# A packed attention with FFN: the last four pairs of units of batch 1 by seven block products, signs of weights with one operand, and a new order of the early steps

## The chip, the cores and the metric

The kernel runs on one core of one Trainium2 chip. The time is the device time of one execution in microseconds; the comparison is between the medians of several executions of either kernel on the same chip.

## What is computed

Eight batches of eight heads, 576 tokens of 64 elements a head. A first attention lets 32 packs a head attend to the tokens; a second lets the tokens attend to the packs. The result, 4608 tokens of 512 elements, goes through an FFN of width 2048 with a gated activation, all in float32:

```python
def _attn_ref(q, k, v, p):
    p_packed = sm_attn(p, k, v)
    out = sm_attn(q, p_packed, p_packed)

def _moe_ref(x, w_in, w_out):
    h = x @ w_in
    g = h * (1.0 / (1.0 + np.exp(-h)))
    return (g @ w_out).astype(np.float32)
```

The kernel never forms the attention's result: it multiplies the packs by w_in first ("packs", one matrix of 128x512 a parity and quarter of the FFN) and then multiplies these by the shares of the second softmax.

## The kernel before, in words

**Weights.** w_in and w_out arrive as 64-bit numbers in 20 chunks (eight of 512 columns, one FFN block each; twelve of 1024), on SP's queue (`Weights.fetch`, L269). Each is put together as float32 from its upper and lower words: ScalarE scales the upper word (`scale`, L283) and rounds the lower (`round`, L287), VectorE bounds the upper (`bound`, L291), puts the sign into the lower (`sign`, L295), shifts (`shift`, L303), and VectorE or GpSimd adds the two (`join`, L306). w_out is then split into an upper and a lower part (`upper`, `lower`). w_in stays in `win`, four quarters.

**A product in float32** is made of three faster products, upper by upper, upper by lower, lower by upper. The first three units of batch 0 (`WHOLE`) use plain float32 matmuls instead, so that no splits are needed yet.

**Units.** A unit is one batch and one block of 128 of the FFN's 2048. `h_products` (L797) multiplies packs by shares, `h_values` (L813) applies the gated activation, `h_lower` (L848) makes the lower part, and `out_part` or `out_products` multiply by w_out and add up in `ps_acc` over a batch's units (L853 to L914). 256 of a half's 288 tokens go through a unit; the other 32 are put aside in `rest` and have units of their own. Units 0 to 31 are those of batches 0 and 1, in the order of `BLOCKS`: batch 0's first two quarters, batch 1's first two, batch 0's last two, batch 1's last two (units 24 to 31). Units 32 to 35 are the rest of both; from unit 36 on the batches follow one another.

**Seven block products.** From batch 2 on, two neighbouring units form a pair (`Seven`, L677): two blocks of the FFN by two halves of the tokens by two parities is a product of 2x2 matrices of blocks, and seven products in place of eight give it. For this, sums and differences of blocks of the packs are made in place (`sums`, L693; step `mv` on VectorE, `mp` on GpSimd), split (`parts`, L704, step `mh`), and the shares get block differences of their own (`blocks2`, `parts2`, steps `aP`, `aQ`). Steps H, I, J, K, L (L733 to L757) issue the seven products into three banks of `ps_one`, with copies on ScalarE and additions on VectorE between them; A and B (`values`, L761) apply the activation to the even and the odd half.

**Packs.** `Packs.products` (L635) makes a quarter's packs. With `kept` (L659) they are stored over the quarter of `win` that they came from, and `split` (L665) makes upper and lower parts from there; `packs_split` (L1000, step `Kd`) makes the parts straight from PSUM and stores nothing. Before that the first half of each quarter of w_in is copied to `spare` in DRAM (step `c`) and is loaded again (step `wb`) for the next batch's packs.

**PSUM.** Up to step `za` there are two tiles of two banks for scores and units (`ps_two`); from there on four single banks (`ps_one`). Four banks are `ps_acc`. Step `zb` frees the weights' staging room for `late`, `odd`, `gp_b` and `s1p`.

**The order** is written out by hand as a string, `ORDER` (L54): each step names a helper and its numbers, and each engine, SP's queue included, takes its instructions in that order. `W` are warm-up matmuls; `k`, `v`, `q` load a batch's inputs; `as` to `aj` are the first attention, `aS` to `aL` the second; `w.` the weights (`wf` fetch, `ws`, `wr`, `wz`, `wg`, `wt`, `wj` in the order of the sentence above, `wu` and `wl` the split); `pp`, `pu`, `pl` packs and their split; `h`, `g`, `l`, `o` a unit; `O` one output block; `e` storing a batch's rows; `b` loading partial sums. `SEVENS` says which pairs of which batch go by sevens.

Of the kernel before, what the change touches and what calls it, by code (L numbers as in the profile page):

```python
# [1090 lines left out]
```

## Time and profile before

| | before |
|---|---|
| median of 3 runs | 677.47 us (677.41 to 678.12) |
| the profiled execution's own time | 677.38 us |
| its span | 675.6 us |
| TensorE, VectorE, ScalarE, GpSimd busy | 666.2, 447.5, 461.1, 75.4 us |
| LDWEIGHTS busy | 542.8 us |
| DMA | 77.76 MB, mean 115 GB/s |

PE is TensorE, PEld its loading of weights, DVE VectorE, ACT ScalarE, POOL GpSimd, SP the engine that issues the DMAs. Busy time is the time in which an instruction of that engine runs. Matmuls are pipelined and their ends are modelled: two neighbouring rows can overlap, and the distance between their starts is the better measure. Releasers of waits are inferred from semaphores. Line numbers are those of the kernel before. The granted clock of TensorE is 1.00 in every stretch shown.

### The profile page before, as it was taken

The numbers are of one execution on the slowest core, as the hardware profiler recorded it, in microseconds if no ns is written. First come the engines' busy times: TensorE is split into PE (matmuls) and PEld (weight loads), VectorE is DVE, ScalarE is ACT, GpSimd is POOL, SyncE is SP. The second block draws the span as 40 slices with busy tenths as digits, with TensorE's granted clock in tenths as the row PEclk, the third lists the DMA queues.
The fourth block names the chain that finished last, engine by engine and source line by source line (L and its number), as shares of the span: only waits on it lengthen the run. The fifth ranks groups of instructions, "written<-read, shape, count | busy, mean of one in ns | idle before, by whom it ended". The sixth has DMA issues, their size and how long they took to land.

```text
span 675.6 us, 12742 instructions
## 1 busy us (share of the span) xinstructions
PE 666.2 (99%) x4920; PEld 542.8 (80%) x4920; DVE 447.5 (66%) x784; ACT 461.1 (68%) x1060; POOL 75.4 (11%) x79
## 2 busy tenths in 40 slices
PE   8999999999999999999999999999999999999997
PEld 5558888868888778886888868887788868888886
DVE  3999977656655788655685479755668566955431
ACT  4999786555648686765777578766677657776542
POOL 1122013110300000211001220212002101001000
PEclk9999999999999999999999999999999999999999
DMA  9966527605214420247011320184202330110002
GB/s 356 420 225 251 198 103 216 244 1 205 104 64 141 147 108 1 65 143 268 18 62 52 95 103 1 40 260 146 85 26 74 84 121 1 31 64 1 1 0 79
DMA packets 31916, 77.76 MB, mean 115 GB/s; under 512 B 17136, under 2 KB 17136, under 8 KB 27504
## 3 DMA queue, kind: packets, MB, share of 16 engines
q1 hardware_dynamic: 31760, 76.82, 32.3%
q8 instruction: 39, 0.64, 0.4%
q10 hardware_dynamic: 96, 0.13, 0.1%
q14 instruction: 21, 0.17, 0.1%
HBM read 59.77 MB, written 13.63 MB: 109 GB/s over the span
## 4 chain that ended last, share of the span: by engine, by line
PE 95%; DMA 3%; ACT 2%; issue 0%; DVE 0%; SPq 0%; ACTq 0%
PE ps_acc L862 59%; PE ps_one L730 20%; PE ps_two L811 5%; PE ps_one L338 5%; PE ps_one L811 2%; DMA win<-in_w_in 2%; PE ps_two L338 1%; PE ps_one L434 1%; DMA kvq_t<-in_pkT 1%; PE ps_two L434 0%; ACT win L663 0%; ACT s L369 0%; ACT L840 0%; PE ps_two L408 0%; ACT pw_hi L672 0%
## 5 line engine op out<-in xcount | busy, mean ns | idle before, releaser
L862 PE MATMUL ps_acc<-wo_hi,g_hi 128*128 128x512 f32 x564 | 223.1, 396 | 0.0
L862 PE MATMUL ps_acc<-wo_lo,g_hi 128*128 128x512 f32 x564 | 221.0, 392 | 0.0
L862 PE MATMUL ps_acc<-wo_hi,g_lo 128*128 128x512 f32 x564 | 220.1, 390 | 0.0
L862 PEld LDWEIGHTS ps_acc<-wo_hi,g_hi 128*128 128x128 f32 x564 | 105.9, 188 | 23.5 <-issue 8.6
L862 PEld LDWEIGHTS ps_acc<-wo_hi,g_lo 128*128 128x128 f32 x564 | 105.9, 188 | 23.5
L862 PEld LDWEIGHTS ps_acc<-wo_lo,g_hi 128*128 128x128 f32 x564 | 105.9, 188 | 14.0
L748 DVE TENSOR_TENSOR top<-ps_one,top 128x288 f32<-128x288 f32 x48 | 21.8, 455 | 57.1 <-ACT top L747 56.8
L699 POOL TENSOR_TENSOR win<-win 128x256 f32<-128x256 f32 x15 | 12.1, 808 | 421.0 <-DVE pw_lo L673 247.2
L777 DVE TENSOR_TENSOR g_lo<-low,g_hi 128x512 fp32r<-128x512 f32 x48 | 33.9, 707 | 34.5 <-ACT low L769 34.5
L747 ACT COPY top<-ps_one 128x288 f32<-128x288 f32 x48 | 19.1, 398 | 46.8 <-PE ps_one L730 46.6
L743 ACT COPY low<-ps_one 128x288 f32<-128x288 f32 x48 | 19.2, 400 | 34.8 <-PE ps_one L730 33.1
L777 DVE TENSOR_TENSOR g_lo<-top,g_hi 128x512 fp32r<-128x512 f32 x48 | 33.9, 707 | 11.8 <-ACT top L775 10.7
L730 PE MATMUL ps_one<-wide_hi,odd 128*128 128x288 f32 x144 | 38.2, 296 | 0.2 <-ACT top L738 0.2
L774 ACT ACTIVATE g_hi<-top 128x512 fp32r<-128x512 f32 x48 | 30.4, 633 | 11.0 <-DVE top L748 8.8
L755 DVE TENSOR_TENSOR low<-ps_one,low 128x288 f32<-128x288 f32 x48 | 21.7, 452 | 24.2 <-PE ps_one L730 23.1
L851 DVE TENSOR_TENSOR g_lo<-g,g_hi 128x512 fp32r<-128x512 f32 (+1 forms) x30 | 21.5, 716 | 19.3 <-ACT g_hi L836 9.7
L775 ACT ACTIVATE top<-top 128x512 f32<-128x512 f32 x48 | 30.4, 633 | 1.5
L673 DVE TENSOR_TENSOR pw_lo<-win,pw_hi 128x512 fp32r<-128x512 f32 (+1 forms) x50 | 26.6, 557 | 3.2 <-ACT pw_hi L672 2.5
L730 PE MATMUL ps_one<-a_hi,pw_hi 128*128 128x288 f32 x96 | 28.4, 296 | 0.1
L730 PE MATMUL ps_one<-a_hi,pw_lo 128*128 128x288 f32 x96 | 28.2, 294 | 0.0
L730 PE MATMUL ps_one<-a_lo,pw_hi 128*128 128x288 f32 x96 | 28.2, 294 | 0.0
L730 PEld LDWEIGHTS ps_one<-wide_hi,odd 128*128 128x128 f32 x144 | 26.3, 188 | 2.1 <-ACT top L738 0.5
(236 smaller groups left out, 1445.6 us busy)
## 6 DMA issues: line engine op xcount, KB each, us to landing
win<-spare SPq DMA_DIRECT2D x21, 512.0 KB, 3.8
kvq_t<-in_v SPq DMA_DIRECT2D x8, 1280.0 KB, 7.3
kvq_t<-in_pkT SPq DMA_DIRECT2D x7, 1216.0 KB, 10.3
out<-o SPq DMA_DIRECT2D x16, 512.0 KB, 3.1
kvq_t<-in_qT SPq DMA_DIRECT2D x7, 1152.0 KB, 6.3
w_raw<-in_w_in SPq DMA_DIRECT2D x6, 1024.0 KB, 9.1
win<-in_w_out SPq DMA_DIRECT2D x3, 1024.0 KB, 6.2
w_raw<-in_w_out SPq DMA_DIRECT2D x3, 1024.0 KB, 6.8
```

The costliest lines, as they stand in the source:

```text
L338: nc.tensor.matmul(bank(par)[NP * i : NP * i + NP], lhs(r, i), rhs(r, i), start=True, stop=True)
L673: nc.vector.tensor_tensor(some_lo, some, some_hi.bitcast(F32), ALU.subtract)
L730: nc.tensor.matmul(bank, x, y, start=(first and n == 0), stop=(n == 2), skip_group_check=True)
L743: nc.scalar.copy(self.low[:, 0], self.x)
L748: nc.vector.tensor_tensor(self.top[:, 1], self.z, self.top[:, 1], ALU.add)
L755: nc.vector.tensor_tensor(self.low[:, 0], self.z, self.low[:, 0], ALU.add)
L774: nc.scalar.activation(g_hi.rearrange("p (n s) -> p n s", n=2), g, AF.Silu)
L775: nc.scalar.activation(g, g, AF.Silu)
L777: nc.vector.tensor_tensor(g_lo.rearrange("p (n s) -> p n s", n=2), g, g_hi.bitcast(F32).rearrange("p (n s) -> p n s", n=2), ALU.subtract)
L811: nc.tensor.matmul(bank, p[:, par, cols] if u >= WHOLE else p[:, par], a[:, par], start=(n == 0), stop=(n == len(todo) - 1))
L851: nc.vector.tensor_tensor(g_lo[:, c], g[:, c], g_hi[:, c].bitcast(F32), ALU.subtract)
L862: nc.tensor.matmul(bank, g[:, rows], w[:, at], start=(first and n == 0), stop=(last and n + 1 == len(todo)))
```

## The change

The pairs of units 24 to 31 of batch 1 go by seven block products. For that the third quarter's packs of batch 1 are kept, in a tile of `s1p` and not over `win`, so that this quarter needs no new load for batch 2. Batch 1 gets the sums of its shares' parts (step `aR1`) and their block differences (`aP1`, `aQ1`). `sign` becomes an operation with one operand on 16-bit words. The order is another one up to the middle of batch 2 (686 steps of before become 699); from step `aH3.1` in batch 3 on it is the same, 1003 steps.

```diff
-SEVENS = [()] * EARLY + [range(8)] * (B - EARLY)
+SEVENS = [(), range(4, 8)] + [range(8)] * (B - EARLY)

+    def room_of_packs(b, j):
+        if b >= EARLY or j != 2:
+            return over_win(j).bitcast(F32)
+        if ("room", b) not in made:
+            made["room", b] = s1p.tile([P, 2 * S], F32, name="s1")[:, : 2 * DM].rearrange("p (r e) -> p r e", r=2)
+        return made["room", b]

+            halves = raw.bitcast(U16).rearrange("p (n four) -> p four n", four=4)
+            self.halves[n] = halves[:, 1], halves[:, 3]

         def sign(self, n):
-            low, up = self.raw[n]
-            nc.vector.scalar_tensor_tensor(low, up, -(2**31), low, op0=ALU.bitwise_and, op1=ALU.bitwise_or)
+            low, up = self.halves[n]
+            nc.vector.tensor_scalar(low, up, 2**15, None, op0=ALU.bitwise_and)

-            self.whole = [over_win(j)[:, par].bitcast(F32) for par in range(2)]
+            self.whole = [room_of_packs(self.b, j)[:, par] for par in range(2)]
...
-            elif self.n < 4 or self.n == 5 and self.b < EARLY:
+            elif self.n < 4:
                 t = s1p.tile([P, 2 * S], F32R, name="s1")[:, : 2 * DM]
```

`sums` and `parts` use `room_of_packs` in the same way. Of the order, the first lines and the stretch from step `za` to batch 2's first pair, before:

```
W7 k0 as0.0 W1 wf0 v0 as0.1 am0.0 am0.1 W4 ax0.0 W3 W1 W1 wr0 at0.0 ay0.0 ax0.1 ar0 at0.1 ws0 wz0 wt0 wg0 wj0 ay0.1
wf1 wr1 aa0 an0 ai0 aj0 q0 wf2 wf3 W1 aS0.0 ws1 wz1 wg1 wt1 wj1 aC0.0 aS0.1 aC0.1 aB0.0 ws2 wr2 wf4 aB0.1 aM0.0 aE0.0
aX0.0 pp0 aM0.1 pu0 k1 wf5 wr4 W14 wf6 aD0.0 wf7 ws3 ws4 aE0.1 aG0.0 wf8 aX0.1 wz2 aD0.1 wr3 aU0.0 aF0.0 aH0.0 as1.0
ac1.0 wt2 aG0.1 wg2 h0.0 as1.1 aU0.1 wj2 g0.0 wz4 wg4 ws6 wz3 aF0.1 wf9 wt3 pp1 q1 wg3 wj3 pu1 ws5 wt4 ac1.1 am1 wj4
wr6 wz6 o0.0 h1.0 g1.0 ws8 wz5 wt5 v1 wz8 aL0.0 wt6 wr5 wg5 wg6 h0.1 g0.1 h1.1 g1.1 wj5 o1.0 o0.1 ax1.0 ax1.1 at1.0
...
aj2 za O20.0.0 O20.1.0 O20.1.1 Kp1.3 Ke1.3 Kp1.2 wu19 O20.0.1 O21.0.0 wl19 zb h22 g22 b0 l22 Kd1.2 O21.0.1 h23 O21.1.1
g23 q2 aS2.0 aT2.0 aY2 Kp2.0 Ke2.0 Kp2.1 Ke2.1 l23 Kp2.2 aM2.0 aS2.1 Ke2.2 O22.0.0 aT2.1 O22.1.1 h24 O21.1.0 h25
...
O36.0.0 O36.1.1 O37.0.0 O36.1.0 k4 wb2.0 ax3.0 ax3.1 O36.0.1 L38 O37.1.1 O38.0.1 at3.0 K38 at3.1 O37.0.1 ar3 O39.1.0
```

and after:

```
W7 k0 as0.0 as0.1 W4 W3 v0 am0.0 wf0 ax0.0 am0.1 W1 W1 at0.0 ay0.0 ax0.1 at0.1 ar0 ay0.1 aa0 an0 ws0 wz0 ai0 wr0 wg0
wt0 wj0 q0 aj0 aS0.0 wf1 wf2 aC0.0 aS0.1 aC0.1 wf3 W1 ws1 aB0.0 aM0.0 aE0.0 k1 pp0 pu0 aB0.1 W14 aX0.0 aM0.1 wf4 wf5
wf6 wr2 aD0.0 aG0.0 aE0.1 ws2 wz2 wg2 wf7 aU0.0 wr3 wt2 wz1 wj2 wt1 ws3 wr1 wg1 wj1 aF0.0 aX0.1 aH0.0 as1.0 ac1.0
as1.1 ac1.1 aD0.1 aG0.1 wr4 wz3 pp1 pu1 ws5 wz5 h0.0 wt3 wt5 g0.0 h1.0 g1.0 wf8 aU0.1 ws4 wz4 wt4 wg4 aF0.1 wg3 wj3
wr7 wj4 am1 q1 aL0.0 ws7 wz7 wg7 wr5 wg5 o0.0 h1.1 wj5 g1.1 h0.1 ws6 wz6 wt6 pp2 g0.1 pu2 ax1.0 o1.0 wt7 wj7 ax1.1 ar1
h2.0 at1.0 ws8 ay1.0 wz8 wr8 o0.1 at1.1 o1.1 v1 wg8 ay1.1 aa1 wf9 wt8 wj8 an1 g2.0 h2.1 wr6 wu7 wg6 wj6 ws9 wl7 ai1
...
wl19 h21 o19 g21 l21 za O20.1.0 aR1 aP1 h22 O20.0.0 zb g22 l22 Kp1.2 Ke1.2 aQ1 Kp1.3 O21.1.0 Ke1.3 O20.1.1 h23 Ks1.2
O20.0.1 O22.1.1 g23 l23 b0 q2 aS2.0 aT2.0 mv1.4 Kp2.0 Ke2.0 aS2.1 aT2.1 O21.1.1 mh1.4 O22.1.0 O23.1.0 O23.1.1 e23.1
Kp2.1 Kp2.2 Ke2.1 aM2.1 Ke2.2 aY2 aM2.0 H24 I24 O22.0.1 J24 aE2.0 Ks1.3 O21.0.0 O21.0.1 L24 K24 O22.0.0 aE2.1 O23.0.0
A24 mh1.5 B24 O23.0.1 H26 I26 e23.0 O25.1.0 O25.1.1 aX2.0 J26 mv1.6 O24.1.1 O24.0.0 aX2.1 O24.0.1 O24.1.0 A26 O25.0.1
O25.0.0 L26 aD2.0 mh1.7 mh1.6 K26 O27.1.1 O26.0.0 B26 H30 I30 O26.0.1 aG2.0 O27.1.0 J30 O27.0.1 O26.1.1 L30 A30 aD2.1
K30 B30 H28 O27.0.0 O31.1.1 I28 O30.1.1 O31.0.0 aG2.1 J28 aH2.1 aL2.1 O31.0.1 O30.1.0 wb2.3 aH2.0 aL2.0 O30.0.1 L28
...
Kp2.3 Ke2.3 Ks2.3 ar3 k4 aV3 mv2.6 an3 ac4.0 ac4.1 mh2.5 O42.0.1 H44 I44 O41.0.1 ai3 aj3 J44 O40.1.1 O40.1.0 q3 L44
O43.1.0 am4 O42.0.0 K44 O42.1.0 A44 mh2.6 O42.1.1 wb2.0 wb2.1 B44 aS3.0 aT3.0 Kp3.1 aY3 Ke3.1 Kp3.0 Ke3.0 aM3.0 wb2.2
```

## Rows read from the trace of the kernel before

**Rows 1.** The page: busy us, share of the span and instructions of each engine.

```profile
PE 666.2 (99%) x4920; PEld 542.8 (80%) x4920; DVE 447.5 (66%) x784; ACT 461.1 (68%) x1060; POOL 75.4 (11%) x79
```

**Rows 2.** Waits of TensorE from 24 to 675 us: us in total, times, longest.

```profile
PE ps_two L453 <- ACT g_hi L840: 0.7, 1, 0.7
PE ps_one L730 <- ACT top L738: 0.2, 1, 0.2
```

**Rows 3.** Timeline of TensorE near 166 us: start us, duration us, what.

```profile
165.97 0.39 PE L862 MATMUL ps_acc<-wo_hi,g_lo 128*128 128x512 f32 x1
166.20 0.29 PE L811 MATMUL ps_one<-a_hi,pw_hi 128*128 128x288 f32 x1
166.33 0.29 PE L811 MATMUL ps_one<-a_lo,pw_hi 128*128 128x288 f32 x1
```

**Rows 4.** Busy us by stretch: PE, PEld, DVE, ACT, POOL, clock, DMA share, GB/s.

```profile
20.00:30.00 10.00, 8.69 (x81) 5.10 (x80) 9.45 (x18) 9.57 (x18) 1.18 (x1) 1.00 1.02 417
30.00:40.00 10.00, 10.00 (x127) 5.98 (x126) 8.70 (x21) 9.97 (x21) 1.63 (x2) 1.00 0.86 335
```

**Rows 5.** Groups of VectorE by line and shape: busy us, mean ns of one.

```profile
L748 DVE TENSOR_TENSOR top<-ps_one,top 128x288 f32<-128x288 f32 x48 | 21.8, 455 | 57.1 <-ACT top L747 56.8
...
L715 DVE TENSOR_TENSOR odd<-win,odd 128x512 fp32r<-128x512 f32 x24 | 16.5, 687 | 2.1 <-ACT odd L714 1.7
...
L699 DVE TENSOR_TENSOR win<-win 128x256 f32<-128x256 f32 x9 | 3.8, 418 | 0.0
...
L617 DVE TENSOR_TENSOR tm<-tm 128x288 f32<-128x288 f32 x6 | 3.2, 528 | 0.2
```

**Rows 6.** Busy us by stretch, two later stretches, columns as in rows 4.

```profile
140.00:200.00 60.00, 60.00 (x407) 49.51 (x406) 39.56 (x61) 32.32 (x82) 6.87 (x8) 1.00 0.28 105
240.00:260.00 20.00, 20.00 (x153) 15.29 (x138) 17.88 (x35) 16.54 (x36) 0.00 (x0) 1.00 0.09 29
```

**Rows 7.** Timeline of all engines in the first 24 us.

```profile
3.82 0.44 SPq L247 DMA_DIRECT2D rest<-in_qT  x1
...
6.17 0.77 PE L232 MATMUL ps_two<-ident 128*128 128x128 f32 x2
...
6.87 0.72 PE L338 MATMUL ps_acc<-kvq_t 64*32 64x288 f32 x16
...
7.71 0.33 SPq L238 DMA_DIRECT2D kvq_t<-in_pkT  x1
...
9.41 0.67 ACT L289 ACTIVATE w_raw<-w_raw 128x512 int32<-128x512 uint32 x1
...
9.97 0.73 ACT L389 ACTIVATE tm<-ps_acc,nm 128x576 f32<-128x576 f32 x1
...
14.71 0.77 PE L338 MATMUL ps_acc<-rest,ppT 64*32 64x320 f32 x16
...
20.09 0.90 DVE L540 TENSOR_TENSOR tm<-ps_acc,on_tokens 128x768 f32<-128x768 f32 x1
...
20.90 0.68 DVE L574 TENSOR_TENSOR tm<-tm,on_tokens 128x512 f32<-128x512 f32 x1
...
22.81 0.72 PE L338 MATMUL ps_two<-kvq_t 64*32 64x288 f32 x16 [0.46 <-ACT w_raw L289]
```

**Rows 8.** Issue to landing in the first 45 us: queries (L247), then keys (L238).

```profile
DMA to landing us min/median/max: 9.8/10.3/10.8
...
DMA to landing us min/median/max: 4.0/5.0/15.0
```

**Rows 9.** Lines of sign (L297) and bound (L293): ns min/median/max, first and last start, shapes.

```profile
L297 DVE SCALAR_TENSOR_TENSOR w_raw<-w_raw x13: 686/1224/1244, 12.3 to 130.1; 128x1024 int32<-128x1024 int32 x9, 128x512 int32<-128x512 int32 x4
...
L293 DVE TENSOR_SCALAR w_raw<-w_raw x13: 422/687/694, 11.4 to 129.4; 128x1024 f32<-128x1024 f32 x9, 128x512 f32<-128x512 f32 x4
```

**Rows 10.** The page's DMA issues: count, KB each, median us to landing.

```profile
win<-spare SPq DMA_DIRECT2D x21, 512.0 KB, 3.8
...
kvq_t<-in_qT SPq DMA_DIRECT2D x7, 1152.0 KB, 6.3
```

More of the change, by code (lines that the diff above doesn't have):

```diff
@@ L13 @@
 U32 = mybir.dt.uint32
+U16 = mybir.dt.uint16
 I64 = mybir.dt.int64
@@ new lines @@
+O69.0.1 J72 O70.1.0 g71 l71 O70.1.1 L72 O70.0.1 A72 O70.0.0 O71.0.0 mh4.1 K72 O71.0.1 B72 wb4.0 O71.1.0 H74 I74
+O73.1.1 O72.1.1 J74 O71.1.1 O73.1.0 e71.0 L74 O72.0.1 O72.0.0 O73.0.1 ay5 mh4.2 K74 A74 O74.0.1 B74 H76 mh4.3 I76
+O74.0.0 O72.1.0 wb4.3 O75.1.1 O75.0.0 J76 O74.1.1 ar5 O73.0.0 O75.1.0 L76 K76 Ks4.2 mp4.4 A76 B76 O75.0.1 H78 O74.1.0
+I78 O77.1.0 O76.0.0 J78 O77.1.1 O76.0.1 L78 wb4.1 A78 K78 B78 O76.1.0 O77.0.1 Kp4.3 Ke4.3 Ks4.3 mp4.6 aV5 mh4.4 an5
+ac6.0 ac6.1 mh4.5 O79.1.1 O79.1.0 am6 H80 I80 ai5 O78.0.1 J80 aj5 O78.0.0 mh4.7 O77.0.0 q5 L80 O76.1.1 K80 A80 B80
@@ new lines @@
+mh5.1 wb5.0 v6 A88 e87.1 O86.0.0 O86.0.1 O87.0.1 e87.0 K88 L88 B88 H90 O88.0.1 O88.0.0 mh5.2 O89.1.0 k7 I90 O89.0.0
+O88.1.0 J90 O89.0.1 O89.1.1 L90 A90 K90 O88.1.1 B90 H92 O90.0.0 mh5.3 I92 O91.0.1 O91.1.1 J92 Ks5.2 mp5.4 O91.1.0
+O90.0.1 L92 O90.1.1 A92 O90.1.0 K92 B92 O91.0.0 H94 I94 O92.1.1 O93.0.1 mh5.4 J94 A94 wb5.3 O92.0.1 O92.1.0 O93.0.0
+L94 K94 O93.1.0 B94 O95.1.0 Kp5.3 Ke5.3 Ks5.3 mp5.6 ay6 aV6 an6 ac7.0 ac7.1 O94.0.0 H96 q6 am7 I96 mh5.5 O95.1.1
+O92.0.0 J96 O95.0.0 ai6 O93.1.1 wb5.1 mh5.7 aj6 L96 O94.1.1 A96 O94.0.1 K96 B96 O97.1.0 O94.1.0 aS6.0 aT6.0 aY6 wb5.2
@@ new lines @@
+O120.0.1 aL7.1 mh7.0 J122 O120.1.1 aH7.0 aL7.0 aP7 O119.0.0 K122 A122 O121.0.1 O121.0.0 O121.1.0 O121.1.1 L122
+O123.1.0 O122.0.1 O122.0.0 aQ7 B122 H124 Ks7.1 I124 O123.0.0 O123.0.1 mh7.1 J124 O120.1.0 O122.1.0 e123.0 K124 L124
+O123.1.1 A124 B124 O122.1.1 H126 e123.1 O125.1.1 mv7.2 I126 O125.1.0 O124.0.1 J126 O124.1.0 O125.0.0 O124.0.0 A126
+L126 mh7.3 mh7.2 O125.0.1 O126.0.0 K126 B126 O127.1.1 H128 I128 Ks7.2 mp7.4 O127.1.0 O124.1.1 J128 O126.1.0 O126.0.1
+L128 A128 K128 O127.0.0 B128 O126.1.1 H130 I130 O129.1.1 O129.0.0 O127.0.1 J130 A130 O128.0.1 O128.0.0 O129.0.1 L130
@@ L141 @@
+e139.0 O139.1.1 l140 O140.1.0 O140.0.0 O140.1.1 g142 l142 O142.0.1 e139.1 O140.0.1 g143 l143 g141 O142.1.1 O143.1.1
+O143.1.0 l141 O141.1.1 O143.0.1 O141.0.0 O141.0.1 O142.1.0 O143.0.0 O142.0.0 O141.1.0 e143.0
 """
-SEVENS = [()] * EARLY + [range(8)] * (B - EARLY)
+SEVENS = [(), range(4, 8)] + [range(8)] * (B - EARLY)
 WAYS = dict(b11=(0, 0), b21=(0, 1), b12=(1, 0), b22=(1, 1), t1=(2, 0), t4=(2, 1), t3=(2, 2), t2=(2, 3))
@@ L266, in __init__ @@
         def __init__(self, stage):
-            self.stage, self.raw = stage, {}
+            self.stage, self.raw, self.halves = stage, {}, {}
         def fetch(self, n):
@@ L279, in fetch @@
             nc.sync.dma_start(raw.bitcast(I64), (w_in if inner else w_out)[:, f * DM : (f + nf) * DM])
-            raw = raw.rearrange("p (n two) -> p two n", two=2)
-            self.raw[n] = raw[:, 0], raw[:, 1]
+            words = raw.rearrange("p (n two) -> p two n", two=2)
+            halves = raw.bitcast(U16).rearrange("p (n four) -> p four n", four=4)
+            self.raw[n] = words[:, 0], words[:, 1]
+            self.halves[n] = halves[:, 1], halves[:, 3]
         def scale(self, n):
@@ L695, in sums @@
                 n = 2 if self.n % 2 == 0 and (self.b, self.n + 1) in sevens else 1
-                both = over_win(self.n // 2).bitcast(F32)[:, :, self.n % 2 * 2 * P : (self.n % 2 + n) * 2 * P]
+                both = room_of_packs(self.b, self.n // 2)[:, :, self.n % 2 * 2 * P : (self.n % 2 + n) * 2 * P]
                 (a11, a21), (a12, a22) = [[both[:, par].rearrange("p (g k n) -> p g k n", g=n, k=2)[:, :, k] for k in range(2)] for par in range(2)]
```

143 lines of the change are left out of this document (56 added, 87 removed).

## The prediction

> **What bounds the kernel now.** I read the profile's page first. TensorE is busy 666.2 of 675.6 us [rows 1], but its matmuls are pipelined and their ends are modelled, so this share alone settles nothing. Next come TensorE's waits from 24 us to the end: 0.7 and 0.2 us, each once, and nothing else [rows 2]. Then the timeline inside a stage: a matmul of 288 columns is followed 0.13 us later by the next one, one of 512 columns 0.23 us later, though each is listed as taking 0.29 or 0.39 us [rows 3]. So from about 23 us on TensorE takes matmuls back to back, and the time is the moment at which that stream starts plus the sum of its spacings. Before it comes a start-up, a chain through batch 0's attention; beside it VectorE and ScalarE are 9.45 and 9.57 of 10 us busy from 20 to 30 us, 8.70 and 9.97 in the next ten [rows 4]. So three things can move the time: fewer matmuls, an earlier start, and new waits of TensorE.
>
> The rule against this reading: LDWEIGHTS takes 542.8 us, 80% of the span [rows 1]. The Trainium skill ("Perfetto Trace Analysis", Identifying the Most-Contended Engine) says that TensorE's matmul occupancy is no measure and that LDWEIGHTS busy share tells its headroom; by that, a fifth of the span is free and a removed matmul need not show. The spacings decide for me: no room stands between matmuls [rows 3].
>
> **Part 1, seven products for pairs of batch 1.** Units 24 to 31 are four pairs. A pair of plain units issues 24 matmuls of 288 columns (2 halves x 2 parities x 3 terms, twice), a pair by sevens 7 x 3 = 21. So 4 x 3 = 12 matmuls go, each worth its spacing, 0.131 us [rows 3]: **-1.57 us**. Output matmuls and the packs' products are as many as before.
>
> What it adds lies on VectorE and ScalarE. On VectorE, per pair: three additions of 128x288 (0.455 each) and one lower part of 128x512 (0.69) [rows 5], 2.05 us, times 4 is 8.2. Two calls of the block sums, four operations of 128x256 at 0.418 each [rows 5]: 3.3. For the shares of batch 1: two additions and two subtractions of 128x576, estimated at 0.77 each by length from 0.69 for 512, 3.1; four block differences at 0.53 [rows 5], 2.1. Together **16.7 us**; the values' lower parts are as many as before, and keeping the third pack instead of splitting it at once adds about nothing, since half a split falls away. ScalarE gets some 8 us (three copies at about 0.4 and one at 0.63 a pair), but from 140 to 200 us it is busy 32.3 of 60, so I price that at nothing; uncovered, a late copy would hold a PSUM bank for at most its own 0.4 us.
>
> VectorE has no such cover. In this stretch, which holds the eight units and the lead-up to batch 2's sevens, it is busy 39.56 of 60 us [rows 6]. The demand becomes 56.3 in 60 - 1.6 = 58.4 us, 96%. The best that rows show over ten busy microseconds is 9.45 of 10 [rows 4]: 56.3/0.945 = 59.6, so TensorE waits **+1.2 us**. The lower end is 0, by 240 to 260 us, where VectorE runs at 17.88 of 20 and TensorE shows no wait [rows 6, 2]; the upper end is +5.6, if it gets no more than 88%. I take the row of the fullest stretch, which this one is nearest to. Queued behind a late VectorE addition are the fourth and fifth products, which go into the banks it reads, and the next pair's first products, which need its lower part.
>
> **Part 2, the start.** The keys' second half takes 5.0 us to land [rows 8]; TensorE then does a warm-up first (6.17) and the scores at 6.87 [rows 7]; the warm-up goes behind them, 0.6 us. ScalarE rounds a w_in chunk (9.41) ahead of the second exponential (9.97) [rows 7]; the rounding goes behind, 0.6 us. The second scores need the queries, issued 3.82, landed 10.8 us later, 14.6, and start at 14.71 [rows 7, 8]. In the new order one w_out chunk of 512 KB is behind them on SP's queue instead of ahead; at 417 GB/s [rows 4] that is 1.26 us. So all three inputs of the second scores come about 1 us earlier. Later, VectorE does half 1's subtraction (20.09) ahead of half 0's scaling (20.90) [rows 7]; exchanged, 0.9 us. Batch 1's keys, issued 7.71, take 15.0 us, 22.7, and their scores start at 22.81 [rows 7, 8]: again one chunk fewer ahead, 21.5.
>
> Against that: the first FFN products now stand behind both of batch 1's scores and the second pack, and that pack needs a weight chunk that VectorE finishes among six weight operations, put ahead of half 1's scaling. So not all of 1.3 to 2 us arrives. I take **-1.0 us**, half of the way from the end -2.0 (every step counts) to 0; the other end is +0.7, if VectorE's six operations (about 0.43 each, 2.6 us) eat more than the start wins.
>
> **Part 3, signs with one operand.** A sign operation with two operands takes 0.69 us for 512 columns, 1.22 for 1024 [rows 9]. No row shows a 16-bit operation with steps of four. The nearest one-operand row with steps is the bound: 0.42 for 512, 0.69 for 1024 [rows 9]. I take that: 8 x 0.26 + 12 x 0.54 = 8.6 us off VectorE up to 130 us, with both ends 0 and that. None lies on TensorE's stream; it pays for the six operations of part 2. The one long wait after 24 us, 0.7 us at the table load for the gated values near 41 us [rows 2], should shrink, since what it waits for moves forward: **-0.5 us**, ends -0.9 and +0.5. The number of table loads stays.
>
> **Moved transfers.** Queries 1 and values 1 pass the w_out chunk 9, which lands some 6 us later (1.18 + 1.31 MB ahead of it at 417 GB/s); its first user on ScalarE moved behind the first values of unit 2, so nothing waits. Values 2 go behind four steps of the weights, keys 3 ahead of queries 2: SP waits for a buffer that is free by then. The reloads of packs' room 0 and 1 for batch 3 move from far ahead to just before their use, behind queries 3 on SP. Landing takes 6.3 us for queries and 3.8 for a reload [rows 10], about 9 us for the three queued; TensorE has some 8.6 us of work in between. Up to 0.4 us; inside the +1.2.
>
> **Sum.** -1.57 - 1.0 - 0.5 + 1.2 = -1.9 on the profiled execution's own 677.38 (span 675.6 and 1.8 around it), 675.5; the median of the runs is 0.09 above it, so **675.6**.
>
> **Rivals.** A measurement here tells about 0.2%, 1.35 us, from no change.
>
> *The start gives nothing (0.22).* For it: ScalarE is 9.97 of 10 busy from 30 to 40 us [rows 4], and none of its work there goes. Then parts 2 and 3 are 0: 677.47 - 1.57 + 1.2 = 677.1, no change.
>
> *VectorE becomes the bound (0.16), slower.* Place: from the switch of PSUM pools to batch 2's first seven. At 88% it needs 56.3/0.88 = 64.0 us for 58.4, +5.6; with the gains, 677.47 - 3.07 + 5.6 = 680.0. It decides at a wait of 3.07 + 1.35 = 4.4 us, a VectorE share under 90%. For it: the largest share without a wait that I see is 89%, over 20 us only. Against: VectorE is lighter just before, and can run ahead.
>
> *The signs are no cheaper (0.05).* If steps of four in 16 bits cost as two operands do, half of the start is eaten: 677.47 - 1.57 - 0.5 - 0.5 + 1.2 = 676.1, within 0.2%: the change does not do what it says.
>
> *TensorE has slack (0.04).* Then the 12 matmuls are worth nothing: 677.47 - 1.0 - 0.5 + 1.2 = 677.2. This is the case that the page's rule on LDWEIGHTS would make.
>
> **How the numbers follow.** The forecast has 0.53, and all of it is faster. Same: 0.22 + 0.05 + 0.04 = 0.31. Slower: 0.16. The low end is 677.47 - 1.57 - 2.0 - 0.9 = 673.0, with VectorE keeping up; the high end, 679.0, takes in the three rivals near 677 and the milder part of the slower one, a wait up to 4.6 us. The likeliest case's own range is 673.0 to 676.1.
>
> **What would show it.** Right: 12 fewer matmuls of 288 columns; batch 1's first scores near 21.5; TensorE's waits from 24 us still under 2 us; VectorE over 90% from 140 to 200 us; signs at 0.43 and 0.69. Wrong: TensorE waiting for VectorE additions or lower parts by more than 3 us in that stretch, or the first block of FFN products no earlier than now.

## The result and the profile after

The changed kernel takes **686.42 us** (median; 685.15 to 686.75) against 677.5 for the kernel before: ratio 1.0125, 95% interval 1.011 to 1.014. It is 8.9 us slower; the forecast was 675.6, and its range ended at 679.0. The profiled execution's span is 685.0, 9.4 more than before.

The page's first part, against [rows 1]: 14 matmuls fewer (12 of the units, 2 of a warm-up), VectorE 21 us busier, ScalarE 7.

```profile
PE 668.1 (98%) x4906; PEld 541.8 (79%) x4906; DVE 468.8 (68%) x817; ACT 468.2 (68%) x1075; POOL 74.5 (11%) x79
```

TensorE's waits from 24 to 675 us, against [rows 2] (0.7 and 0.2, no more): us in total, times, longest.

```profile
PE ps_two L822 <- ACT rest L855: 2.5, 2, 2.2
PE ps_one L741 <- ACT s L380: 1.8, 1, 1.8
PE ps_acc L873 <- DVE o L939: 1.2, 1, 1.2
PE ps_acc L530 <- DVE tm L585: 1.2, 1, 1.2
PE ps_one L741 <- ACT top L749: 0.5, 2, 0.3
PE ps_two L349 <- DVE win L319: 0.3, 1, 0.3
PE ps_two L822 <- DVE pw_lo L668: 0.3, 1, 0.3
PE ps_two L349 <- POOL win L319: 0.3, 1, 0.3
```

These are 8.1 us, and none of them falls between 140 and 194 us, where the pairs of units 24 to 31 are. Where the time went is read best from the start of one and the same step in TensorE's timelines (us; the last two kernels are runs of the next section):

| step | before | after | late_old | best2_plain |
|---|---|---|---|---|
| as1.0, batch 1's scores | 22.82 | 21.53 | 21.61 | 22.73 |
| aU0.1, half 1 turned back | 25.18 | 26.95 | 26.42 | 25.09 |
| o2.0 | 42.72 | 42.72 | 42.22 | 42.63 |
| o7 | 67.13 | 68.87 | 68.33 | 67.05 |
| h20 | 127.28 | 133.84 | 131.64 | 127.18 |
| as3.0 | 188.35 | 193.69 | 192.67 | 188.75 |
| H44 | 231.24 | 240.00 | 235.58 | 233.73 |
| H60, past all changes of order | 305.73 | 314.91 | 310.05 | 308.69 |

The column late_old is of that kernel's fastest execution, 681.75 us; its other three took 683.71 to 683.97. At aU0.1 the two kernels with the new early order have already done the second pack and the products h1.0, which stand behind it before.

The changed kernel is level at o2.0, 1.7 late at o7, **6.6 late at h20**, 5.3 at as3.0 (the matmuls saved lie in between) and 9.2 at H60. From o2.0 to o7 TensorE's waits are three, of 0.3, 0.3 and 0.2 us; the rest of that 1.7 is not explained. Three places of its timeline show where the start's gain and most of the other losses went.

**The start.** VectorE signs weight chunk 1 (L308) ahead of half 1's sum (L569) and scaling (L585); TensorE waits for the scaling.

```profile
20.11 0.62 PE L530 MATMUL ps_acc<-ident,tm 128*128 128x128 f32 x4
21.53 1.21 PE L349 MATMUL ps_two<-kvq_t 64*32 64x288 f32 x32 [0.80 <-DMA kvq_t<-in_pkT]
23.40 0.75 DVE L308 TENSOR_SCALAR w_raw<-w_raw 128x512 uint16<-128x512 uint16 x1
23.92 0.93 DVE L569 TENSOR_REDUCE on_tokens<-tm 128x24 f32<-128x768 f32 x1
25.93 0.96 DVE L585 TENSOR_TENSOR tm<-tm,on_tokens 128x768 f32<-128x768 f32 x1
26.94 0.44 PE L530 MATMUL ps_acc<-ident,tm 128*128 128x128 f32 x2 [1.21 <-DVE tm L585]
```

**Weight chunk 15, 110 to 120 us.** This is a chain through four engines, to be read from the top. VectorE is not full here, 15.23 of 20 us from 100 to 120 us, but it stands idle for 2.30 us at the bound of chunk 18, whose transfer landed late (ScalarE's scaling of it waits for the DMA until 109.72). Only behind it come the signs of 18 and 15 (2.53) and the shifts (1.30), then GpSimd's joins, then the upper half of chunk 15 on ScalarE, which had waited 3.34 us, then the activation queued behind that (L855 is its last part), and TensorE gets its banks. Chunk 18's transfer was issued at 103.89; whether an earlier issue would have spared the wait as well, no run tests.

```profile
109.72 1.12 ACT L296 ACTIVATE w_raw<-w_raw 128x1024 f32<-128x1024 f32 x1 [2.48 <-DMA w_raw<-in_w_out]
...
110.87 0.70 DVE L304 TENSOR_SCALAR w_raw<-w_raw 128x1024 f32<-128x1024 f32 x1 [2.30 <-ACT w_raw L296]
...
111.95 2.53 DVE L308 TENSOR_SCALAR w_raw<-w_raw 128x1024 uint16<-128x1024 uint16 x2 [0.38 <-ACT w_raw L300]
...
114.52 1.30 DVE L315 TENSOR_SCALAR w_raw<-w_raw 128x1024 int32<-128x1024 int32 x2
...
115.34 4.52 POOL L319 TENSOR_TENSOR w_raw<-w_raw 128x1024 int32<-128x1024 int32 x2 [11.48 <-DVE w_raw L315]
...
117.59 1.14 ACT L335 CAST wo_hi<-w_raw 128x1024 fp32r<-128x1024 f32 x1 [3.34 <-POOL w_raw L319]
...
119.39 0.38 PE L822 MATMUL ps_two<-a_hi,pw_hi 128*128 128x256 f32 x1 [2.22 <-ACT rest L855]
```

Right behind this wait the windows (columns as in [rows 4]; the first is the one of VectorE's 15.23) show TensorE at a granted clock of 0.57, for the most part at 1.2 GHz in place of 2.4:

```profile
100.00:120.00 20.00, 17.78 (x106) 14.10 (x105) 15.23 (x17) 11.48 (x19) 7.19 (x3) 1.00 0.70 240
116.00:120.00 4.00, 1.78 (x11) 1.24 (x10) 3.33 (x3) 2.41 (x5) 3.86 (x2) 1.00 0.32 54
120.00:124.00 4.00, 4.00 (x16) 3.57 (x15) 2.94 (x4) 1.40 (x3) 0.00 (x0) 0.57 0.65 212
```

**Batch 3's scaling, 239 us.** Four block sums (L710 to L713) stand ahead of the scaling (L455) on VectorE; ScalarE's copies wait for it, and TensorE for the copies.

```profile
238.88 0.42 DVE L713 TENSOR_TENSOR win<-win 128x256 f32<-128x256 f32 x1
239.23 0.28 DVE L455 TENSOR_TENSOR pp<-ps_one,rd 128x128 f32<-128x128 f32 x1
239.54 1.31 ACT L380 COPY s<-ps_one 128x288 f32<-128x288 f32 x4 [2.94 <-DVE pp L455]
...
239.99 0.40 PE L741 MATMUL ps_one<-a_hi,pw_hi 128*128 128x288 f32 x1 [1.77 <-ACT s L380]
```

The signs, line L308, against [rows 9]: dearer than with two operands, not cheaper (ns min/median/max).

```profile
L308 DVE TENSOR_SCALAR w_raw<-w_raw x13: 748/1333/1399, 13.4 to 134.2; 128x1024 uint16<-128x1024 uint16 x9, 128x512 uint16<-128x512 uint16 x4
L308 DVE TENSOR_SCALAR win<-win x7: 740/776/1350, 28.9 to 86.4; 128x512 uint16<-128x512 uint16 x4, 128x1024 uint16<-128x1024 uint16 x3
```

### The profile page after: what moved, and what is told of

It is laid out like the page before. It is cut to its first block, busy times and chain, and to the rows that moved or that the text cites. A ratio compares the mean times of both kernels' runs of the same rounds, so it can differ in the third digit from the quotient of the medians.

```text
span 685.0 us, 12758 instructions
## 1 busy us (share of the span) xinstructions
PE 668.1 (98%) x4906; PEld 541.8 (79%) x4906; DVE 468.8 (68%) x817; ACT 468.2 (68%) x1075; POOL 74.5 (11%) x79
## 4 chain that ended last, share of the span: by engine, by line
PE 77%; ACT 2%; DVE 2%; DMA 1%; SPq 1%; issue 1%; POOL 0%; ACTq 0%; DVEq 0%
PE ps_acc L873 50%; PE ps_one L741 21%; PE ps_one L349 5%; DMA e1T<-tm 1%; PE ps_two L822 1%; PE ps_one L445 1%; DVE pw_lo L684 0%; PE ps_one L822 0%; ACT s L380 0%; ACT win L674 0%; SPq L428 0%; ACT pw_hi L683 0%; POOL w_raw L319 0%; DVE a_lo L612 0%; DVE w_raw L308 0%
## 5 line engine op out<-in xcount | busy, mean ns | idle before, releaser
L759 DVE TENSOR_TENSOR top<-ps_one,top 128x288 f32<-128x288 f32 x52 | 23.7, 455 | 62.9 <-ACT top L758 62.5
L788 DVE TENSOR_TENSOR g_lo<-low,g_hi 128x512 fp32r<-128x512 f32 x52 | 36.6, 704 | 34.7 <-ACT low L780 34.6
L710 POOL TENSOR_TENSOR win<-win 128x256 f32<-128x256 f32 x15 | 12.2, 812 | 428.5 <-DVE pw_lo L684 194.1
L788 DVE TENSOR_TENSOR g_lo<-top,g_hi 128x512 fp32r<-128x512 f32 x52 | 36.7, 705 | 12.9 <-ACT top L786 12.0
L741 PE MATMUL ps_one<-wide_hi,odd 128*128 128x288 f32 x156 | 42.0, 298 | 0.5 <-ACT top L749 0.5
L785 ACT ACTIVATE g_hi<-top 128x512 fp32r<-128x512 f32 x52 | 32.9, 633 | 12.4 <-DVE top L759 8.6
L786 ACT ACTIVATE top<-top 128x512 f32<-128x512 f32 x52 | 32.9, 633 | 1.7
L741 PE MATMUL ps_one<-a_hi,pw_hi 128*128 128x288 f32 x104 | 31.0, 298 | 1.9 <-ACT s L380 1.8
L741 PE MATMUL ps_one<-a_hi,pw_lo 128*128 128x288 f32 x104 | 30.6, 294 | 0.0
L741 PE MATMUL ps_one<-a_lo,pw_hi 128*128 128x288 f32 x104 | 30.6, 294 | 0.0
L684 DVE TENSOR_TENSOR pw_lo<-win,pw_hi 128x256 fp32r<-128x256 f32 (+1 forms) x50 | 26.9, 563 | 2.6 <-ACT pw_hi L683 2.0
L750 DVE TENSOR_TENSOR top<-ps_one,top 128x288 f32<-128x288 f32 x52 | 23.4, 450 | 6.2 <-ACT top L749 5.6
```

The lines of the kernel that those rows point to most:

```text
L684: nc.vector.tensor_tensor(some_lo, some, some_hi.bitcast(F32), ALU.subtract)
L741: nc.tensor.matmul(bank, x, y, start=(first and n == 0), stop=(n == 2), skip_group_check=True)
L750: nc.vector.tensor_tensor(self.top[:, 0], self.y, self.top[:, 0], ALU.add)
L759: nc.vector.tensor_tensor(self.top[:, 1], self.z, self.top[:, 1], ALU.add)
L785: nc.scalar.activation(g_hi.rearrange("p (n s) -> p n s", n=2), g, AF.Silu)
L786: nc.scalar.activation(g, g, AF.Silu)
```

## The experiments

The theory from these traces: the seven products gain what they save; the new order costs, because steps stand on VectorE's and ScalarE's queues ahead of what TensorE waits for. The rivals: the sign operation costs; VectorE is full with the seven products. In the edits below only the steps concerned are written.

### Which part costs

**sign_alone**: the kernel before, with the new `sign` and nothing else.

```diff
-            nc.vector.scalar_tensor_tensor(low, up, -(2**31), low, op0=ALU.bitwise_and, op1=ALU.bitwise_or)
+            nc.vector.tensor_scalar(low, up, 2**15, None, op0=ALU.bitwise_and)
```

> The kernel before with the new sign operation and nothing else. In the changed kernel's trace the one-operand sign takes 0.75 us for 512 columns and 1.33 for 1024, against 0.69 and 1.22 with two operands. Theory (the new order is what costs): 20 signs by 0.06 to 0.11 are about 2 us of VectorE before 130 us, part of it behind cover, so +0.5 to +1.5 us on 677.5. Rival (the sign is what costs): some +5 us or more, for then most of the 8.9 us must be here.

677.92 us, ratio 1.0004 (0.9995 to 1.0014); the span is 675.6 as before. The sign costs nothing that shows: +0.4 between the medians, -0.3 to +0.9 by the interval, under or at the lower end of the theory's range. The rival's +5 falls.

**early_old**: the changed kernel with the order before up to step `za`. Two pieces that the later order expects by then were put in by hand:

```diff
-aj2 za
+wu19 wl19 k3 aj2 za
```

> The changed kernel with the order of the kernel before up to the switch of the PSUM pools at about 135 us; signs, seven products and everything later stay as changed. Theory (two thirds of the loss is the early order): the lead at the switch falls from +6.6 to the signs' +0.5 to +1.5, and the later part still costs its net +2.5, so 680 to 682 us. Rival (VectorE is full in the stretch with the seven products, and that is the bound): no better than 684.5, since the early loss would only come back as waits later.

688.1 us, ratio 1.0153 (1.0136 to 1.017): a miss, by the edit's own order. At h20 the kernel is 0.6 late, not 6.6. But the piece put in, chunk 19's upper half (L334), waits for GpSimd's join, and the packs' copy (L467) stands behind it on ScalarE, which TensorE needs at once; it waits 4.4 us. The timeline of ScalarE in this run:

```profile
137.82 1.11 ACT L334 CAST wo_hi<-w_raw 128x1024 fp32r<-128x1024 f32 x1 [3.38 <-POOL w_raw L318]
138.83 0.26 ACT L467 COPY ppT<-ps_two 128x128 f32<-128x128 f32 x1
```

One step set ahead of another made 4.4 us: the mechanism that I claim for the change, by accident.

**late_old**: the changed order and signs up to `za`, then the order before, without the seven products. Keys 3 (`k3`) and the halves of chunk 19 (`wu19 wl19`) stand behind `za`, where the order before has them.

```diff
-SEVENS = [(), range(4, 8)] + [range(8)] * (B - EARLY)
+SEVENS = [()] * EARLY + [range(8)] * (B - EARLY)
```

> The changed kernel's order and signs up to the switch of the PSUM pools at about 135 us, and from there the order of the kernel before, without seven products for batch 1. Theory (early order): the +6.6 us of lead at the switch stay to the end, 683.5 to 684.5 us. Rival (the seven products are what costs): near 678 to 680.

683.78 us, ratio 1.0084 (1.0069 to 1.01): as expected. **The early order costs 6.2 us by itself**, the new signs included, which sign_alone puts at +0.4. The profiled execution took 681.75, the other three 683.71 to 683.97; in its trace TensorE waits 2.27 us for the same activation, and the clock stays up:

```profile
120.00:124.00 4.00, 4.00 (x21) 3.39 (x20) 2.43 (x5) 1.54 (x5) 0.00 (x0) 1.00 0.77 263
```

The mean granted clock of this execution is 0.999, that of the other three 0.996 to 0.997; no trace shows where in them it fell. So of the 6.2 some 2 us go with the clock, and 4.2 are left where it stays up.

**sevens_off**: the changed kernel with plain units 24 to 31 in the same places.

```diff
-aR1 aP1 aQ1 Ke1.2 Ks1.2 mv1.4 mv1.6 mh1.4 mh1.5 mh1.6 mh1.7 H24 I24 J24 L24 K24 A24 B24
+Kd1.2 h24 h25 g24 l24 g25 l25
```

> The changed kernel with units 24 to 31 as plain units in the same places of the order: twelve matmuls of 288 columns come back (12 by 0.131, +1.57 us) and some 16.7 us of VectorE go from 140 to 200 us. Theory (the order is what costs, and the seven products gain what they save): the one wait near 194 us that stands behind VectorE shrinks by about 1.3, so 686.5 to 688 us. Rival (VectorE full): the waits of 140 to 200 us go, 684 us or less.

688.15 us, ratio 1.0159 (1.0144 to 1.0174), at the upper edge. Between the medians the seven products save 1.7 us in the changed kernel, about the 12 matmuls' 1.57. The two intervals (up to 1.014, from 1.0144) only just lie apart, but the traces agree: from h20 to as3.0 the changed kernel takes 59.85 us and this run 61.28, 1.4 more. The windows of the changed kernel and of this run from 140 to 200 us:

```profile
140.00:200.00 60.00, 58.78 (x414) 46.27 (x413) 51.98 (x90) 38.22 (x93) 7.36 (x8) 1.00 0.15 53
```

```profile
140.00:200.00 60.00, 58.53 (x418) 46.43 (x417) 36.24 (x55) 28.52 (x73) 7.38 (x8) 1.00 0.15 53
```

VectorE has 15.7 us less to do, and TensorE stands as much: its wait near 194 us is 1.5 instead of 1.2. In this order VectorE's load is not what it waits for.

### Mending the order step by step

**c15_first**, chunk 15 ahead of chunk 18 on VectorE:

```diff
-wz15 v2 o13 ws18 wr18 g16 wz18 wg18 c3 wg15 wt15 wj15 ws17 wu15
+wz15 wg15 wt15 wj15 v2 o13 ws18 wr18 g16 wz18 wg18 c3 ws17 wu15
```

> The changed kernel with one edit: the sign, the shift and the join of weight chunk 15 stand right behind its bound, ahead of the scaling, rounding, bound and sign of chunk 18. In the changed kernel VectorE is idle for 2.30 us at 110.9 (its queue stands at chunk 18, whose transfer has landed late) while chunk 15 waits behind it; the join, the weight's upper half on ScalarE, the activation behind that and TensorE's banks follow late. Theory (queue order): the join starts some 4 us earlier, TensorE's wait at 117 us (2.4) goes, and with it the stretch at half clock behind it (some 2.0 us): 682 to 684 us. Rival (the sign or VectorE's whole load delays chunk 15 anyway): 686 or more, with the wait still there.

685.63 us, ratio 1.0112 (1.0095 to 1.0129): a miss of the size, and the 0.8 us gained are within the noise. In the trace the edit does what it was meant to: the wait at 117 us and the slow stretch behind it are gone, and h20 starts at 129.34 instead of 133.84, 4.5 earlier. Then 1.7 is given back by h22: ScalarE's copy of the packs and an activation are late at the switch (new waits of 0.5 and 0.8), and 2.75 is left at H44. In the profiled execution the other long wait, at 237 us, now has the slow stretch behind it, and 1.25 is left at H60. The window where the wait was, TensorE now busy all through it, and the slow one, clock 0.61:

```profile
116.00:120.00 4.00, 4.00 (x24) 3.59 (x23) 3.19 (x4) 2.50 (x6) 1.26 (x1) 1.00 0.34 59
...
240.00:243.00 3.00, 3.00 (x12) 2.48 (x11) 0.26 (x1) 1.07 (x3) 0.00 (x0) 0.61 0.92 335
```

**an3_first**, batch 3's scaling ahead of the block sums:

```diff
-aV3 mv2.6 an3 ac4.0
+aV3 an3 mv2.6 ac4.0
```

> The changed kernel with one edit: batch 3's scaling by the shares stands ahead of four block sums on VectorE near 238 us instead of behind them. Theory (queue order): the scaling comes 1.7 us earlier, the copies of batch 4's scores on ScalarE that free TensorE's banks with it, and TensorE's wait of 1.8 us there goes: 684 to 685 us. Rival (VectorE full): the time moves to the next wait, 686 or more.

685.02 us, ratio 1.0101 (1.0086 to 1.0116): 1.4 less, at the upper end of what was expected; the wait is 0.3 instead of 1.8.

**early_old2**: early_old with `wu19 wl19` behind `h22 O20.0.0`.

> As the run early_old, with the two halves of the last weight chunk moved from ahead of the third batch's packs to behind the first of its units at the switch, so that the copy of the packs on ScalarE no longer stands behind GpSimd's join (TensorE waited 4.4 us for it in that run). Theory: the early order's loss is gone (+0.6 at the step before the switch in that run) and only the later part's net +2.5 stays: 679.5 to 681 us. Rival (VectorE full in the stretch of the seven products): over 683.

684.39 us, ratio 1.0096 (1.0079 to 1.0113): over the theory's range. The early loss is gone (h20 at 127.54), but from 135 to 141 us TensorE waits again at my seam (1.45 for an activation that stands behind chunk 19's upper half, which waits 3.62 for the join), and as3.0 is 2.2 late.

**mended**: early_old2 with an3_first's edit, and `l32` behind `e31.0`.

> The kernel early_old2 with two more edits: batch 3's scaling ahead of the four block sums near 238 us, and the addition that frees the accumulator near 194 us ahead of a remainder's lower part on VectorE. Theory (queue order): 1.7 and 0.6 us less than early_old2, 677 to 678.5, so that the seven products pay for what is left of the late order's waits. Rival (VectorE full): within 0.5 us of early_old2.

682.5 us, ratio 1.0063 (1.0047 to 1.008): 1.9 less than early_old2, against 2.3 expected. The range of 677 to 678.5 was worked out from what early_old2 was expected to take, and is missed with it. The addition's wait fell from 1.2 to 0.6, but 0.4 came back for the lower part put off, so that most of it is an3's.

**c15_an3**: c15_first and an3_first together.

> The changed kernel with both edits, of c15_first and of an3_first. Theory (two queue orders, and each long wait of TensorE can bring a stretch of 3.4 us at half clock behind it: the run c15_first lost its wait at 114 us and showed such a stretch at 239 us, behind the other wait, instead of at 120 us): with both waits gone the clock stays up, and the gains add to more than the two alone gave (0.8 and 1.4): 686.4 less 2.4 and 2.0 at 114 us, less 1.5 at 237 us, plus 0.5 to 1.3 of new small waits at the switch, 681 to 682 us. Rival (VectorE full; what one wait gives comes back at the next): the sum of the two alone or less, 684 us or more.

684.9 us, ratio 1.0101 (1.0086 to 1.0116): the theory's 681 to 682 is missed, and the time lies where the rival put it. Neither wait is there. TensorE waits 1.0 and 0.8 at the switch, and in the profiled execution a slow stretch stands at 28 us, behind the start's wait of 1.2. The two edits gave 0.8 and 1.4 alone and give 1.5 together, which the noise does not tell from their sum; but the waits and slow stretches that they removed were 5.9 in the traces. What is mended at one place is in large part lost again at the next.

**c15_an3_d**: c15_an3 with batch 2's differences `aP2` moved from behind `Ks2.1` to behind `A28`.

> The kernel c15_an3 with one more edit: batch 2's four block differences stand on VectorE before the split of the packs that sets GpSimd's block sums going, instead of behind it. In the changed kernel three of the four take 0.88 us beside GpSimd and the first 0.45 without, and the addition that frees the accumulator at 194 us stands behind them. Theory (queue order): 1.3 us less VectorE ahead of that addition, TensorE's wait of 1.2 us there goes, 0.6 to 1.3 us less than c15_an3. Rival (VectorE full from 180 to 200 us): the addition comes no earlier, same time.

683.47 us, ratio 1.0081 (1.0065 to 1.0097). The addition's wait falls from 1.2 to 0.2; but GpSimd's sums start later, and the first pair of batch 2 has a new wait of 0.8. The profiled execution has no slow stretch, but it is the slowest of the four (684.2), with a wait of 2.1 for the packs' copy at the switch. So what the 1.4 us between the medians come from is not shown; the mean granted clock is 0.997 to 1.0 over the four executions, against 0.995 to 0.998 in c15_an3.

### Does anything beat the kernel before?

**best**: the order before through the switch, then the changed one with c15_an3_d's and an3's edits.

```diff
-za O20.1.0 aR1 aP1 h22 O20.0.0 zb g22 l22 Kp1.2 Ke1.2 aQ1 Kp1.3 O21.1.0 Ke1.3 O20.1.1 h23
+za O20.0.0 O20.1.0 aR1 O20.1.1 Kp1.3 Ke1.3 Kp1.2 wu19 O20.0.1 O21.0.0 wl19 aP1 zb h22 Ke1.2 aQ1 g22 l22 O21.1.0 h23
```

> The order of the kernel before up to and through the switch of the PSUM pools (packs ahead of the first units, as there), then the changed kernel's order with the seven products, the block differences early and batch 3's scaling ahead of the block sums. Theory: the early loss (4.4 at 114 to 122 us, some 1 at 42 to 65) and the loss at the seam that early_old2 showed (2.9) are gone; what stays of the late part is 1.7 of small waits over the kernel before against 1.57 saved, so 677 to 679 us. Rival (VectorE full with the seven products): 680.5 or more.

682.37 us, ratio 1.0069 (1.005 to 1.0088): the rival's side of the line. TensorE stands at h23 for the copy of batch 1's packs, which VectorE does behind the shares (0.5, and 0.8 right behind it).

**part1_alone**: the order before throughout, pairs set in by hand (`H24 I24 ... B24` for `h24 h25 g24 l24 g25 l25`, and so on).

> Part 1 alone: the kernel before with its order and its signs up to the switch of the PSUM pools, and from there its own order with the plain units 24 to 31 replaced by four pairs by seven products (third pair last), the additions and lower parts for them set in where VectorE is idle before their users. Twelve matmuls of 288 columns fewer (-1.57 us), some 15.7 us more of VectorE from 140 to 200 us (the difference of the runs with and without the seven products in the changed order). Theory (the products gain what they save where the queues' order lets them): 676 to 678 us, with TensorE's waits between 135 and 200 us under 2 us. Rival (VectorE becomes the bound, the slower case of the forecast): 680 us or more, with TensorE waiting for additions and lower parts of the pairs.

696.35 us, ratio 1.0276 (1.0262 to 1.029): neither. VectorE is busy 10.31 of 20 us from 160 to 180. ScalarE waits 5.76 us for an output's transfer, because the pair's odd parts (L724) go into the room of that output; all its queue stands behind that, and TensorE waits 5.3. It waits another 5.2 for ScalarE's copies into `top`, and the granted clock is 0.82 from 160 to 180 us and 0.92 in the next twenty. So this run prices the places that I chose by hand, and not part 1 alone:

```profile
163.72 0.62 ACT L724 CAST o<-s 128x512 fp32r<-128x512 f32 x1 [5.76 <-DMA out<-o]
```

**start_first**: `wz1 wt1 wg1 wj1` behind `aG0.1`, in the changed kernel.

> The changed kernel with one edit in the start: bound, shift, sign and join of weight chunk 1 stand behind batch 0's scaling of the second half on VectorE, instead of ahead of its sum. In the changed kernel TensorE starts batch 0's first half at 20.1 us against 21.7 before, but waits 1.2 us for that scaling (25.9 to 26.9 us), which had come at 24.0 to 24.9 before. Theory (the order ate the start's gain): the wait of 1.2 goes; but VectorE is busy 9.83 of 10 us from 20 to 30 us, so chunk 1 is then late for the first output products, and at 42 us at most 0.5 us is left: 685.9 to 686.5. Rival (the start's gain is real and only one step hides it): 1.2 us earlier at 42 us and 685.2 or less.

686.13 us, ratio 1.0128 (1.011 to 1.0146): as expected. aU0.1 starts at 25.43 instead of 26.95, and TensorE then waits for the join of chunk 1 instead; o2.0 is at 43.08, no earlier:

```profile
28.44 1.98 PE L872 MATMUL ps_acc<-o,g_hi 128*128 128x512 f32 x4 [1.86 <-POOL o L318]
```

**best2**: best with `aR1` and `aP1` behind the packs' copy, `aP2` back, two-operand signs; `aQ1` goes behind `l23`.

```diff
-Ke1.3 Kp1.2 wu19 O20.0.1 O21.0.0 wl19 aP1 zb h22 Ke1.2 aQ1 g22 l22 O21.1.0 h23 Ks1.2
+Ke1.3 Kp1.2 wu19 O20.0.1 O21.0.0 wl19 zb h22 Ke1.2 aR1 g22 l22 O21.1.0 h23 Ks1.2 aP1
```

> The kernel best with three edits: batch 1's shares are put together and differenced behind the copy of its packs instead of ahead of it (TensorE waited 1.7 us there for that copy, VectorE being busy with the shares), batch 2's differences stand back behind the packs' split, where the changed kernel has them (ahead of it GpSimd's sums came 1.05 us late for the first seven), and the signs have two operands. Theory (queue order): 1.7 to 2.5 us less than best, 680 to 681; not under the kernel before, since the late order's waits near 150 to 200 and at 236 us, about 4, stay against 1.57 saved. Rival (VectorE full in 140 to 160 us, 18 of 20 busy): the same 1.7 us comes back behind the shares, 682 or more.

683.66 us, ratio 1.0095 (1.0078 to 1.0112): the rival's result. The wait came back at the next users, as 2.1 us for a copy on ScalarE that stands behind the shares' parts, which wait for VectorE's differences (L629).

```profile
PE ps_one L348 <- ACT tm L481: 2.1, 1, 2.1
```

**best2_plain**: best2 with plain units 24 to 31, as in sevens_off.

> The kernel best2 with plain units 24 to 31, without batch 1's shares put together and without block sums for it, in the same places of the order: 1.57 us of matmuls more, 15.7 us of VectorE less. In best2 TensorE loses 4.75 us from 135 to 150 us (0.89 in the kernel before) and has a stretch at half clock behind its longest wait. Theory A (VectorE's steps for the seven products are what TensorE waits for there, where no early loss covers them): most of that loss and the half clock go, 1.57 comes back, 679.5 to 681.5 us. Theory B (the order of the steps around the switch is to blame, the products are not): the loss stays, 684 us or more.

680.54 us, ratio 1.0041 (1.0026 to 1.0055): **theory A**. The windows of best2 and of this run from 140 to 150 us: VectorE 9.66 against 5.20, TensorE 7.86 against 10.00. ScalarE's load falls too, from 6.52 to 3.67; that VectorE is the one waited for is read from the chain in best2.

```profile
140.00:150.00 10.00, 7.86 (x75) 5.16 (x74) 9.66 (x20) 6.52 (x16) 0.00 (x0) 0.91 0.01 2
```

```profile
140.00:150.00 10.00, 10.00 (x113) 6.46 (x112) 5.20 (x10) 3.67 (x11) 0.00 (x0) 1.00 0.01 2
```

In best2, where TensorE comes to the switch on time, the seven products cost 3.1 us net (683.66 - 680.54), so 4.7 with their matmuls; in the changed kernel, where it comes 6.6 us late, they gain 1.7. Of the 4.7 some 2 us go with the clock: it is 0.91 in best2 from 140 to 160 us (an estimate: 0.09 of 20 us) and 1.00 without the products. In best, whose trace shows no lower clock, the net price is 1.8 (682.37 - 680.54; the signs and the place of `aP2` differ too), so that it seems to depend on the order as well. And without any early loss and without the products the later part of the new order still costs 2.6, with batch 3's scaling already mended as in an3_first. No version here beats the kernel before.

## Why the prediction was wrong

**The sum left out most of the order.** The change reorders the steps up to 245 us; I costed it at two ends, the start and a table load, and under "Moved transfers" at "up to 0.4 us". That is the step that failed. Four kernels, each one part away from the next, measure it: the order up to the switch +6.2 (late_old against the kernel before), the rest of the order with plain units +4.4 (sevens_off against late_old, 688.15 - 683.78), the seven products -1.7 (the changed kernel against sevens_off). Together that is the whole 8.9; each difference is uncertain by 1 to 1.5 us. The prices hold in this sequence only: behind the old early order, and with batch 3's scaling mended, the rest of the order costs +2.6 (best2_plain). I looked at the transfers that moved, and not at the queues of VectorE and ScalarE for what stands behind a step that itself waits. A full engine is not needed for that: where most was lost, VectorE was busy 15.23 of 20 us.

With the order fell the sentence that let me price ScalarE at nothing, that "a late copy would hold a PSUM bank for at most its own 0.4 us". In the changed kernel TensorE stood 2.22 us for an activation on ScalarE and 1.77 for a copy, because the one was queued behind a step that had waited 3.34 us for GpSimd, and the other had itself waited 2.94 for VectorE. Neither is one of the copies that the pairs add.

**Part 1, the products.** The -1.57 was right: -1.7 between sevens_off and the changed kernel. The added load was right too, 15.7 us against 16.7. The +1.2 for VectorE was wrong in the changed kernel: TensorE stands no longer with them than without. Its source was also read too low: 9.45 of 10 is not the fullest stretch of the kernel before, nor is 89% the largest share without a wait, for at 50 to 60 us VectorE runs at 9.65 while TensorE is busy throughout. By that share the sum would have given no wait:

```profile
50.00:60.00 10.00, 10.00 (x73) 8.74 (x58) 9.65 (x15) 9.26 (x14) 2.00 (x1) 1.00 1.01 404
```

**Part 2, the start.** Its inputs came as read: batch 1's scores at 21.53 (forecast 21.5), half 0 turned back 1.6 earlier. The step "I take -1.0 us, half of the way" fell: at o2.0 nothing is left in this trace, and 0.5 in late_old's, whose order is the same up to there. The first block of FFN products, h0.0, starts at 23.74 us against 23.46 before, which the prediction had named as a sign of being wrong. What ate the gain is the mechanism of its other end, the weight operations ahead of half 1's scaling. start_first shows that exchanging these does not bring it back: chunk 1's join is needed as urgently. So for this step the rival "the start gives nothing" was right.

**Part 3, the signs.** "The nearest one-operand row with steps is the bound" was wrong on both sides: 0.75 and 1.33 us, above even the two-operand 0.69 and 1.22. VectorE got some 1.8 us more (8 x 0.06 + 12 x 0.11) instead of 8.6 less. The wait at the table load did go, without any gain at o2.0. The Trainium skill ("VectorE: DVE Perf Modes", Mode 2x_1P) says that two 16-bit values share a read only at a step of one. These operands have a step of four, and the trace agrees in so far as 16 bits bring no gain here.

**The rivals.** The slower one named VectorE, from the switch to batch 2's first seven. In the changed kernel it is not what decides (sevens_off); in best2 it decides just there (best2_plain), at 9.66 of 10 us. That the same load is hidden in one order and costs 4.7 us in the other, the lower clock included, I can show; whether it is TensorE's lateness or the place of the shares ahead of h22 that hides it, I cannot separate. That TensorE has slack, the last rival, is not borne out: twelve matmuls fewer gave about what their spacings add up to.

**Where the theory of the experiments fell short.** An edit can give much less than its wait: c15_first gave 0.8 for a wait of 2.2 and a slow stretch. A queue in order hides the next late step behind the first.

## What to carry to other kernels

When several engines each take their steps in a fixed order, cost a new order by asking of every moved step what is queued behind it on its engine, and whether that step itself waits for a transfer or another engine; a step that waits makes all behind it wait, even on an engine that is far from full. One such place, weight chunk 15, made TensorE 4.5 us later in the trace, where twelve matmuls saved 1.6. Don't add up waits from one trace as gains: mend one, and look for the next. Test a part of a change both beside the rest and without it, since the same extra work can be free in one order and dear in another.

## What was not expected of the hardware

After a wait of 2.2 us TensorE ran at a granted clock of 0.57 over the next 4 us; after 2.27 us at the same place, in another run, at 1.00. Between executions of late_old the time is 681.75 at a mean granted clock of 0.999 and 683.71 to 683.97 at 0.996 to 0.997. In c15_first the stretch stood behind the wait at 237 us, in c15_an3 behind one of 1.2 at 27 us. In the kernel before, with no wait after 24 us over 0.7 [rows 2], the clock is 1.00 in every stretch from 24 to 675 us.

A VectorE operation can take twice as long beside GpSimd's. In the changed kernel's timeline at 189 us the first of four equal differences takes 0.45 us, and the other three, with GpSimd's block sums begun, 0.87 and 0.88 (the second is shown):

```profile
189.55 0.45 DVE L627 TENSOR_TENSOR tm<-tm 128x288 f32<-128x288 f32 x1
189.77 0.83 POOL L710 TENSOR_TENSOR win<-win 128x256 f32<-128x256 f32 x1 [51.35 <-issue]
190.04 0.87 DVE L628 TENSOR_TENSOR tm<-tm 128x288 f32<-128x288 f32 x1
```

And a 16-bit operation with one operand and steps of four is slower, 1.33 us for 1024 columns, than a 32-bit one with two operands and steps of two, 1.22.
